# The plan of an attention and gated MLP kernel on one core: a new order of its steps, fewer fillers on TensorE, two pairs of output rows by eight products, w_out's differences in two parts

## The chip, the core and the metric

One core of a Trainium2 chip. The time is the device's time of one execution in microseconds (us), median of several executions. The engines are named as the profile names them: PE (TensorE matmuls) and PEld (its weight loads), DVE (VectorE), ACT (ScalarE), POOL (GpSimd), SP (SyncE, which issues the DMAs here).

## What is computed

```python
# attention inside chunks of 64 tokens; q, k, v are (8, 8, 576, 64)
scores = scale * np.matmul(q_c, k_c.transpose(0, 1, 2, 4, 3))
attn = np.exp(scores - max); attn = attn / (sum(attn) + 1e-09)
x = matmul(attn, v_c)              # to (8, 576, 512)
# the MLP: d_model 512, d_ff 1024
h = np.maximum(x @ w_in, 0.0)
conv_out = sum over k of conv_w[k] * h shifted by k - 1   # 3 taps along the tokens
gate = 1.0 / (1.0 + np.exp(-conv_out))
return (h * gate @ w_out).astype(np.float32)
```

q, k and v are float32; w_in, conv_w and w_out come as float64 and are split in the kernel into a high and a low part.

## The kernel before

4608 tokens are worked in tiles t0 to t35 of 128 tokens (attention) and in 12 units of 384 tokens (MLP). The kernel first writes down all work as *steps* (`step`, L80): each has an engine, a cost that the planner assumes for it, the steps that it must follow and the buffers that it takes and frees. A step's number is its place in the order of the `step` calls. A list `moved_` (L963) gives some steps to another engine than their first one, and a list `order_` (L991), both written out as numbers, gives the order in which steps are laid. From order and costs a planner (L1089 to L1129) works out a begin for each step, and the steps are emitted by their begins (L1136); so each engine's queue, SP's of DMA issues too, has a fixed order. The begins set nothing else in the chip, except this: where the planner sees PE idle in its first 110 us, it puts in transposes of a unit matrix (*fillers*, L1137 to L1140), one for each 0.14 us of the gap.

**Attention.** `load_rows` (L120) loads q and k of a tile into one of three slots, `load_v` (L171) loads v. For t0 to t8 `t_pe` (L186) turns q and k on PE, `t_copy` (L203) takes them out of PSUM; from t9 on the turning is done by `shuffle`, `load_part` and a transpose on DVE (L217). `scores` (L240) is followed by the softmax: s_max, s_sub (DVE), s_exp (ACT), s_sum, s_eps, s_rec, s_norm (DVE, ACT or POOL), then `p_pe` (PE, L326), `p_copy`, and `attn_v` (PE, L339). `x_hi` and `x_lo` (L394, L398) write x in two parts. From t12 on two tiles are worked together.

**Weights.** `split` (L650) makes of w_in (four pieces of 256 columns, the first two in two halves) a high and a low part: w_scale (ACT, L558), w_shift (DVE, L562), w_words (DVE, L567), w_hi (L76), w_left (L571). `split_o` (L676) does so with w_out and adds four sums and differences of its quarters: w_hi_q and w_lo_q (L584) for the three quarters that are used as they are, w_diff (three instructions, L589 to L591), w_hi_d and w_lo_d (L597) for the four sums and differences.

**MLP.** A block (`block`, L824) is one unit and one of eight slices of 128 hidden columns: `mm1` (12 matmuls, L408), then h_relu, c_mid (L446), c_left and c_right (L451), c_sig (L462), c_mul (L481). The output is made for pairs of 128-token tiles (`pair_steps`, L842; 18 pairs): the 2x2 blocks of h*gate and w_out are multiplied by seven products in place of eight, after Strassen and Winograd. That takes seven *factors* in two parts (f_hi, L76 or L78; f_lo, L499), four sums of blocks (f_sum, L502), seven `product` steps (12 matmuls each, L512) and o_copy, o_both, o_last, o_store. Each product waits for all steps of w_out (`w_all`, L888).

Of the kernel before, what the change touches and what calls it, by code (L numbers as in the profile page):

```python
# [20 lines left out]
F32 = mybir.dt.float32  # L21
F32R = mybir.dt.float32r
U32 = mybir.dt.uint32
# [7 lines left out]
def attn_ffn(ctx: ExitStack, tc: tile.TileContext, q, k, v, w_in, conv_w, w_out, out):  # L31
# [26 lines left out]
    DIRECT = ()  # L58
    scale = 1.0 / float(D) ** 0.5
# [12 lines left out]
    ENG = {"DVE": nc.vector, "POOL": nc.gpsimd}  # L72
# [7 lines left out]
    def step(eng, cost, key, fn, args=(), after=(), take=(), free=(), lag=0.0, port=False, bank=None, other=(), soft=()):  # L80

        s = dict(eng=eng, cost=cost, key=key, fn=fn, args=args, after=[a for a in after if a], take=take, free=free,
                 lag=lag, port=port, bank=bank, other=other, soft=[a for a in soft if a])
        steps.append(s)
        return s
# [28 lines left out]

    def row_slot(st):
        return slots[st["slot"]] if "slot" in st else w_slots[st["wslot"]][:, 0:1024]

    def load_rows(st, t):  # L120
        if t < NP:
            r = row_slot(st).rearrange("(p two) (h c) -> two p h c", two=2, h=H)
            (b0, t0), (b1, t1) = chunk(2 * t), chunk(2 * t + 1)
            for i, src in enumerate((q, k)):
                for b, t_, p0, n in [(b0, t0, 0, C)] if b0 == b1 else [(b0, t0, 0, C // 2), (b1, t1, C // 2, C // 2)]:
                    nc.sync.dma_start(out=r[i, p0:p0 + n], in_=src[b, :, t_:t_ + 2 * n, :].rearrange("h (p e) d -> p h (e d)", e=2))
# [3 lines left out]
        for i, src in enumerate((q, k)):  # L130
            rows = r[:, i].rearrange("p (h d) -> p h d", d=D)
            for b, t_, p0, n in [(b0, t0, 0, P)] if b0 == b1 else [(b0, t0, 0, C), (b1, t1, C, C)]:
                nc.sync.dma_start(out=rows[p0:p0 + n], in_=src[b, :, t_:t_ + n, :].rearrange("h i d -> i h d"))
# [37 lines left out]
    def load_v(st, t):  # L171
# [3 lines left out]
        if t >= TP:  # L175
            (b0, t0), (b1, t1) = chunk(2 * t), chunk(2 * t + 1)
            for b, t_, p0, n in [(b0, t0, 0, P)] if b0 == b1 else [(b0, t0, 0, C), (b1, t1, C, C)]:
                nc.sync.dma_start(out=r[p0:p0 + n].rearrange("p g u d -> p (g u) d"), in_=v[b, :, t_:t_ + n, :].rearrange("h j d -> j h d"))
            return
        (b0, t0), (b1, t1) = chunk(2 * t), chunk(2 * t + 1)  # L180
        for hp in range(2):
            for b, t_, j0, n in [(b0, t0, 0, P)] if b0 == b1 and not hp else [(b0, t0, C * hp, C), (b1, t1, C - C * hp, C)]:
                nc.sync.dma_start(out=r[j0:j0 + n, :, hp, :], in_=v[b, hp::2, t_:t_ + n, :].rearrange("g j d -> j g d"))
# [259 lines left out]

    def c_mid(st, u, f):
# [76 lines left out]
    def o_copy(st, row, col, eng):  # L521
        o, src = o_tile(st)[:, row, col, :], banks[st["y"]][:, 0:DM // 2]
# [10 lines left out]
    def o_last(st):  # L533
        o = st["os"][:, 1, 0, :]
        nc.vector.scalar_tensor_tensor(out=o, in0=banks[st["q"]][:, DM // 2:DM], scalar=0.5, in1=o, op0=ALU.mult, op1=ALU.add)
# [5 lines left out]
    def w_load(st, src):  # L541
        np_, n, m2 = src.shape
        t = w_slots[st["wslot"]].bitcast(U32)[0:np_, 0:n * m2].rearrange("p (n m) -> p n m", m=m2)
        nc.sync.dma_start(out=t, in_=src)
# [41 lines left out]
    def w_diff(st, n, eng):  # L586
        q_ = w_quarters(st, n)
        st["D"] = d = work4.tile([P, 2 * DM], F32, name="wt").rearrange("p (i m) -> p i m", i=4)
# [4 lines left out]
    def w_hi_d(st, n, eng):  # L593
        copy_on(eng, wo_h[:, 3:7, n], st["D"])

    def w_lo_d(st, n, eng):
        ENG[eng].tensor_tensor(out=wo_l[:, 3:7, n], in0=st["D"], in1=wo_h[:, 3:7, n].bitcast(F32), op=ALU.subtract)  # L597
# [50 lines left out]
    slot_users = []  # L648

    def split(key, t_load, src, hi=None, lo=None, half=False):  # L650

        st = {}
        small = hi is None
        a, b, c, p = (0.2, 0.28, 0.35, 0.4) if small else (0.42, 0.68, 0.62, 1.28) if half else (0.69, 1.22, 1.06, 2.35)
        ld = step("SP", 0.55, t_load, w_load, (st, src), take=[("wslot", st)], lag=0.1 if small else 1.6 if half else 3.1)
# [14 lines left out]
        s4 = step("DVE", b, key + 0.01, w_words, (st,), [s2], free=["wslot"], port=True)  # L670
        slot_users.append(s4)
# [4 lines left out]
    def split_o(n, key, t_load):  # L676

        st = {}
        ld = step("SP", 0.55, t_load, w_load, (st, src_o[n]), take=[("wslot", st)], lag=3.5)
# [5 lines left out]
        s6 = step("POOL", 2.95, key + 3, w_diff, (st, n), [s4], take=["wt"], port=True, other=[("DVE", 1.6, True)])  # L685
        s7 = step("POOL", 1.95, key + 4, w_lo_q, (st, n), [s5, s6], free=["wt"], port=True, other=[("DVE", 1.0, True)])
        s8 = step("ACT", 1.06, key + 4, w_hi_d, (st, n), [s6], other=[("POOL", 1.5, True), ("DVE", 0.7, True)])
        s9 = step("POOL", 2.4, key + 5, w_lo_d, (st, n), [s8, s7], free=["wt"], port=True, other=[("DVE", 1.25, True)])
        wo_done[n] = [s5, s7, s8, s9]

    def att(t, key, load_key, writes):

        st = {"t": t}
        if t < NAT:
            r = "slot"
            ld = step("SP", 1.2 if (2 * t) % NCK < NCK - 1 else 2.3, load_key, load_rows, (st, t), take=[(r, st)], lag=1.9 if t < NP else 2.8)
            tt = []
            for i in range(2):
                s = step("PE", 0.9 if t < NP else 0.44, key - 3, t_pe, (st, i), [ld, before.get("t")], take=[("bk", st, ("tp", i))] + ["qk"] * (not i), free=[r] if i else [])
                before["t"] = s  # L700
                tt.append(step("ACT", 0.63 if t < NP else 0.59, key - 3, t_copy, (st, i), [s], free=[("bk", ("tp", i))], other=[("DVE", 0.69, False)]))
            slot_users.append(s)
# [3 lines left out]
        ldv = step("SP", (1.7 if (2 * t) % NCK < NCK - 1 else 2.2) if t < TP else 0.5 if (2 * t) % NCK < NCK - 1 else 1.0, load_key + 0.05 if t < 5 else key - 8, load_v, (st, t), [before.get("v")], take=["v"], lag=1.1 if t < TP else 0.75 if (2 * t) % NCK < NCK - 1 else 1.2)  # L706
# [479 lines left out]
```

## Time and profile before

| | |
|---|---|
| median of 3 executions | 478.6 us (476.5 to 479.18) |
| the profiled execution | 477.3 us |
| its span, first to last instruction | 475.5 us |
| PE busy in the span | 464.0 us (98%) |
| mean granted TensorE clock | 0.996 of full speed |
| first block's first matmul | 39.75 us |
| first product's first matmul | 87.46 us |
| end of the last matmul on the chain | 471.95 us |

A busy PE is not yet a useful one: fillers count as busy. The views used are the page, the busy time by stretch, the chain that ended last, the timeline and the list of instructions by line.

### The profile page before, as it was taken

The page shows a single profiled execution, that of the slowest core. Times are in us where ns is not written, and L with a number is a line of the kernel's source. Part 1 is how long each engine was busy: PE and PEld are TensorE (multiplying, and loading weights), DVE is VectorE, ACT ScalarE, POOL GpSimd, SP SyncE. Part 2 cuts the span into 40 slices and gives each one's busy share as a digit, 9 for nine tenths or more (in the row PEclk, how much of TensorE's full clock was granted, in tenths as well). Part 3 has the DMA queues.
Part 4 walks back from the last instruction along what each step waited for, and adds up shares of the span by engine and source line. Part 5 has one row for each costly group of instructions (what it writes and reads, how often), then busy time and mean ns, then how long its engine had stood idle before and what let it go on. Part 6 is the DMA issues. An engine that isn't in the chain of part 4 may idle for free.

```text
span 475.5 us, 13438 instructions
## 1 busy us (share of the span) xinstructions
PE 464.0 (98%) x5481; PEld 452.9 (95%) x5481; DVE 413.0 (87%) x775; ACT 257.7 (54%) x535; POOL 289.4 (61%) x260
## 2 busy tenths in 40 slices
PE   8989889999999999999999999999999999999996
PEld 8879889999999999999999999999999999999996
DVE  2869999999999898989988999898998998788694
ACT  2557989955555463554564465453545545444631
POOL 0124678976777666767667857467868553633523
PEclk9989999999999999999999999999999999999999
DMA  6878999998789999999938283600361100101002
GB/s 195 237 216 255 282 207 193 188 162 205 133 143 211 200 204 160 157 228 165 221 80 149 60 208 80 166 23 23 102 167 45 46 23 2 46 1 68 8 38 112
DMA packets 186369, 64.33 MB, mean 135 GB/s; under 512 B 159660, under 2 KB 177092, under 8 KB 186308
## 3 DMA queue, kind: packets, MB, share of 16 engines
q1 hardware_dynamic: 186308, 63.48, 61.9%
q8 instruction: 43, 0.70, 0.6%
q14 instruction: 18, 0.15, 0.1%
HBM read 50.88 MB, written 23.59 MB: 157 GB/s over the span
## 4 chain that ended last, share of the span: by engine, by line
PE 89%; DVE 5%; ACT 2%; issue 2%; POOL 1%; POOLq 0%; DVEq 0%
PE b_ps L512 38%; PE b_ps L408 38%; PE sx_ps L247 3%; PE sx_ps L339 3%; PE b_ps L196 2%; PE b_ps L1140 2%; PE z_ps L339 1%; DVE wt L567 1%; PE z_ps L247 1%; PE b_ps L326 1%; DVE gt L451 1%; DVE wt L562 1%; DVE m L257 1%; ACT wt L558 0%; DVE wt L261 0%
## 5 line engine op out<-in xcount | busy, mean ns | idle before, releaser
L512 PE MATMUL b_ps<-wo_h,f 128*128 128x256 f32 x1008 | 190.6, 282 | 0.1
L512 PEld LDWEIGHTS b_ps<-wo_h,f 128*128 128x128 f32 x1008 | 158.6, 188 | 2.2 <-POOL f L78 0.7
L512 PE MATMUL b_ps<-wo_l,f 128*128 128x256 f32 x504 | 141.3, 280 | 0.6 <-issue 0.6
L451 DVE SCALAR_TENSOR_TENSOR gt<-b_ps,cw,gt 128x384 f32<-128x384 f32 (+3 forms) x208 | 116.6, 576 | 9.0 <-ACT gt L446 7.1
L499 POOL TENSOR_TENSOR f<-gt,f 128x512 fp32r<-128x512 f32 x71 | 91.8, 1298 | 29.3 <-ACT f L76 9.8
L512 PEld LDWEIGHTS b_ps<-wo_l,f 128*128 128x128 f32 x504 | 94.9, 188 | 0.3 <-issue 0.3
L408 PE MATMUL b_ps<-x_h,wi_h 128*128 128x386 f32 (+2 forms) x384 | 84.7, 342 | 0.9 <-DVE gb L481 0.9
L408 PE MATMUL b_ps<-x_l,wi_h 128*128 128x386 f32 (+2 forms) x384 | 83.3, 338 | 0.0
L408 PE MATMUL b_ps<-x_h,wi_l 128*128 128x386 f32 (+2 forms) x384 | 83.1, 338 | 0.0
L462 ACT ACTIVATE gt<-gt 128x384 f32<-128x384 f32 (+2 forms) x96 | 50.2, 523 | 43.8 <-DVE gt L451 43.6
L408 PEld LDWEIGHTS b_ps<-x_l,wi_h 128*128 128x128 f32 x384 | 68.8, 188 | 0.0
L408 PEld LDWEIGHTS b_ps<-x_h,wi_l 128*128 128x128 f32 x384 | 68.6, 188 | 0.0
L408 PEld LDWEIGHTS b_ps<-x_h,wi_h 128*128 128x128 f32 x384 | 65.7, 188 | 1.8 <-DVE gb L481 1.2
L446 ACT ACTIVATE gt<-b_ps,cw 128x384 f32<-128x384 f32 (+2 forms) x104 | 56.4, 555 | 18.0 <-DVE b_ps L418 16.3
L416 ACT ACTIVATE b_ps<-b_ps 128x386 f32<-128x386 f32 (+2 forms) x78 | 37.3, 479 | 51.5 <-PE b_ps L408 47.6
L502 POOL TENSOR_TENSOR gt<-gt 128x512 f32<-128x512 f32 x43 | 55.5, 1295 | 15.2 <-PE b_ps L408 6.0
L481 DVE SCALAR_TENSOR_TENSOR gt<-gt,b_ps 128x192 f32<-128x192 f32 (+2 forms) x120 | 47.2, 410 | 8.1 <-ACT gt L462 7.4
L78 POOL CAST f<-gt 128x512 fp32r<-128x512 f32 x42 | 25.8, 613 | 33.9 <-PE b_ps L512 24.1
L76 ACT CAST f<-gt 128x512 fp32r<-128x512 f32 x43 | 26.5, 617 | 25.2 <-PE b_ps L512 14.8
L217 DVE STREAM_TRANSPOSE qkT<-qk 128x1024 f32<-128x1024 f32 (+1 forms) x30 | 33.3, 1119 | 0.4 <-DMA qk<-rows 0.4
L524 ACT ACTIVATE wt<-b_ps 128x256 f32<-128x256 f32 x50 | 18.9, 381 | 24.9 <-PE b_ps L512 24.9
L499 POOL TENSOR_TENSOR f<-gb,f 128x512 fp32r<-128x512 f32 x14 | 18.1, 1294 | 17.8 <-ACT f L76 8.7
(96 smaller groups left out, 614.8 us busy)
## 6 DMA issues: line engine op xcount, KB each, us to landing
out<-wt SPq DMA_DIRECT2D x36, 256.0 KB, 3.7
qk<-rows SPq DMA_DIRECT2D x24, 320.0 KB, 5.0
rows<-in_k SPq DMA_DIRECT2D x12, 576.0 KB, 8.7
rows<-in_q SPq DMA_DIRECT2D x12, 576.0 KB, 8.3
qk<-rows SPq DMA_DIRECT2D x24, 256.0 KB, 4.5
v<-in_v SPq DMA_DIRECT2D x21, 256.0 KB, 5.0
w<-in_moe_w_out SPq DMA_DIRECT2D x4, 1024.0 KB, 6.1
wt<-wt SPq DMA_DIRECT2D x48, 64.0 KB, 2.0
```

Of the source, the lines that this page charges most:

```text
L76: nc.scalar.copy(out=out, in_=in_)
L78: ENG[eng].tensor_copy(out=out, in_=in_)
L217: nc.vector.transpose(out=to[:, :, i:i + n], in_=of[:, :, o:o + n])
L408: nc.tensor.matmul(h_ps[:, 0:w], lhsT=wt[:, f // 2, kt, P * (f % 2):P * (f % 2) + P], rhs=xt[:, u % NX, kt, 0:w], start=n == 0, stop=n == ...
L416: nc.scalar.activation(out=h, in_=h, func=AF.Relu)
L446: nc.scalar.mul(out=g, in_=h, mul=cw[:, FT + f:FT + f + 1])
L451: nc.vector.scalar_tensor_tensor(out=g, in0=h, scalar=w, in1=g, op0=ALU.mult, op1=ALU.add)
L462: nc.scalar.activation(out=g, in_=g, func=AF.Tanh, scale=0.5)
L481: nc.vector.scalar_tensor_tensor(out=o, in0=g, scalar=1.0, in1=hv, op0=ALU.add, op1=ALU.mult)
L499: ENG[eng].tensor_tensor(out=part(st, 1), in0=quarter(*src), in1=part(st, 0).bitcast(F32), op=ALU.subtract)
L502: ENG[eng].tensor_tensor(out=quarter(*out_), in0=quarter(*a), in1=quarter(*b), op=op)
L512: nc.tensor.matmul(o, lhsT=part(ft, a)[:, j, :], rhs=w[:, i, j, :], start=first and n == 0, stop=n == 3 * FT // 2 - 1, skip_group_check=True)
```

## The change

Five things, as the diff has them. (1) `order_` and `moved_` are replaced whole. (2) The planner's account of SP's queue is changed: a transfer is not issued before the eighth one back has landed, and the assumed transfer times (`lag`) differ; this alters only begins. (3) Fillers: a gap gets none if it is no longer than 0.3 us, else one for each 0.115 us beyond 0.3 us and one more; the first gap, from 1.4 us on, gets one for each 0.164 us. (4) `PLAIN = 2`: pairs 0 and 1 are made by eight products of the four blocks themselves. (5) w_out's differences: `w_diff` makes one of the four (128x256), which the plain products use, and the new `w_more` makes the other three; w_hi_d and w_lo_d are split in the same way. Pairs 0 and 1 wait for `wo_done` alone, later pairs for `wo_more` too. The switches `TAPS = 0` and `HOMED = ()` leave the new functions k_* and `home` unused, and every load stays on SP (`eng="SP"`).

```diff
+    PLAIN = 2
+    TAPS = 0
+    HOMED = ()
...
     def w_diff(st, n, eng):
-        ENG[eng].tensor_tensor(out=d[:, 0:2], in0=q_[:, 1::2], in1=q_[:, 0:2], op=ALU.subtract)
-        ENG[eng].tensor_tensor(out=d[:, 2], in0=q_[:, 3], in1=d[:, 0], op=ALU.subtract)
-        ENG[eng].tensor_tensor(out=d[:, 3], in0=q_[:, 2], in1=d[:, 2], op=ALU.subtract)
+        ENG[eng].tensor_tensor(out=st["D"][:, 0], in0=q_[:, 1], in1=q_[:, 0], op=ALU.subtract)
+    def w_more(st, n, eng):
+        ENG[eng].tensor_tensor(out=d[:, 1], in0=q_[:, 3], in1=q_[:, 1], op=ALU.subtract)
+        ENG[eng].tensor_tensor(out=d[:, 2], in0=d[:, 1], in1=q_[:, 0], op=ALU.add)
         ENG[eng].tensor_tensor(out=d[:, 3], in0=q_[:, 2], in1=d[:, 2], op=ALU.subtract)
...
+        if p < PLAIN:
+            ends = [factor(x, at, key + i * d, need(at)) for i, (x, at) in enumerate((("A11", a11), ("A12", a12), ("A21", a21), ("A22", a22)))]
...
+        w_all = [x for n in range(FT // 2) for x in wo_done[n] + ([] if p < PLAIN else wo_more[n])]
...
+        if p < PLAIN:
+            for row, b_ in enumerate("yq"):
+                x = mul(one, 0, at, b_, 0, True, [], [("bk", st, b_)], [])
+                c = copy(row, 1, at, [x, before["st"] if row else None], b_, **({} if row else {"take": ["wt"]}))
+                x = mul(two, 1, at + d, b_, 0, False, [c], [], [])
+                c = copy(row, 0, at + d, [x, c], b_)
+                x = mul(one, 3, at + 2 * d, b_, 1, True, [c])
+                x = mul(two, 2, at + 3 * d, b_, 1, False, [x])
+                e = step("DVE", 0.43, at + 3 * d, o_last, (st, row, 1, b_), [x, c], free=[("bk", b_)])
...
-        if e == "SP":
-            dma_free = max(dma_free, t + 0.3 + cost / 2) + s["lag"]
+        if s["lag"]:
+            ring, x = landed["SP" if e == "ACT" else e], t
+            for j in range(s["m"]):
+                x = max(x, ring[-8 + j]) + cost / s["m"]
...
-            for _ in range(int((begin[i] - pe_free) / 0.14) if idle else 0):
+            wait = begin[i] - pe_free - 0.3
+            for _ in range(int((wait + 0.3) / 0.164) if pe_free < 2.0 else int(wait / 0.115) + 1 if idle and wait > 0 else 0):
                 nc.tensor.transpose(out=banks[idle[-1]][:, 0:P], in_=ident, identity=ident)
```

What the two number lists say, read out as names. On PE up to the first product (t3 is one of a tile's two t_pe, S scores, p p_pe, A attn_v, m02 a block of unit 0 and slice 2):

```
before: t0 t0 t1 S0 t1 t2 c_pe S1 t2 t3 t3 S2 p0 t4 t4 A0 p1 S3 t5 S4 A1 t5 p2 S5 A2 p3 t6 t6
        m00 m02 m07 m03 p4 p5 S6 A3 m04 t7 m05 m06 A5 A4 m01 p6 A6 t7 S7 t8 m13 m10 m12 t8 m14 S8 m16 m11 m17 m15 p7 product
after:  t0 t0 t1 S0 t1 t2 t2 p0 S1 S2 c_pe t3 t3 S3 t4 t4 A0 p1 p2 A1 S4 t5 A2 p3 t5
        m02 S5 m07 p4 t6 t6 m03 t7 S6 t7 m00 p5 S7 A3 m05 m04 p6 A4 m01 m06 A5 A6 t8 t8 p7 S8 m16 m12 m14 m13 p8 A7 m10 A8 m15 m17 m11 product
```

SP's loads start before: rows t0, conv_w, rows t1, t2, half of a w_in piece, rows t3, half, v0, rows t4, half, rows t5, v1, two pieces, v2; after: rows t0, t1, conv_w, rows t2, half, half, rows t3, v0, rows t4, two pieces, v1, rows t5, v2. DVE's steps, before and after, counted in the list: up to the first block t_copy 5 and 2, p_copy 0 and 2, s_max 6 and 5, s_sub 6 and 5, s_sum 5 and 4, s_eps 1 and 4, s_norm 2 and 1, halves of w_shift and w_words 4 and 3; the rest alike. From there to the first product c_left 13 and 12, h_relu 0 and 1, f_lo 1 and 0, s_max, s_sub and s_sum one more each, s_rec 4 and 5, s_eps 0 and 2, s_norm 1 and 0, t_copy 0 and 1, t_dve 1 and 0, w_left of a piece 1 and of a half 0, after the reverse, w_lo_d of four quarters 1 and 0, after one w_diff, w_hi_d and w_lo_d of one quarter, a half of w_shift and w_words 0 and 1, x_lo 4 and 6; the rest alike.

## Rows read from the trace of the kernel before

**Rows 1.** The page: busy time of each engine over the span with its share and instructions, and, from the chain that ended last, its shares by engine.

```profile
PE 464.0 (98%) x5481; PEld 452.9 (95%) x5481; DVE 413.0 (87%) x775; ACT 257.7 (54%) x535; POOL 289.4 (61%) x260
...
PE 89%; DVE 5%; ACT 2%; issue 2%; POOL 1%; POOLq 0%; DVEq 0%
```

**Rows 2.** Busy time by stretch, cut by me at the places that the other groups show. Columns: the stretch, its length, then PE, PEld, DVE, ACT and POOL busy us (instructions), the granted clock, the DMA share and GB/s.

```profile
7.01:23.34 16.33, 16.33 (x441) 14.12 (x441) 11.97 (x24) 6.75 (x13) 1.89 (x2) 1.00 0.85 236
23.34:28.70 5.36, 3.55 (x66) 2.98 (x65) 1.36 (x3) 2.63 (x6) 0.94 (x1) 0.69 0.65 170
28.70:39.70 11.00, 10.27 (x195) 9.44 (x195) 10.43 (x19) 6.66 (x15) 3.52 (x6) 1.00 0.82 248
39.70:62.00 22.30, 21.05 (x241) 20.23 (x240) 21.16 (x40) 20.88 (x40) 13.86 (x14) 1.00 0.98 274
62.00:78.50 16.50, 14.51 (x176) 13.21 (x174) 16.50 (x31) 15.11 (x33) 11.03 (x9) 1.00 1.22 186
78.50:87.40 8.90, 8.90 (x59) 8.85 (x52) 8.56 (x30) 7.58 (x18) 8.74 (x9) 1.00 1.02 224
87.40:130.00 42.60, 42.60 (x593) 41.28 (x592) 38.86 (x86) 26.14 (x57) 33.83 (x31) 1.00 0.94 164
130.00:471.95 341.95, 341.18 (x3696) 337.26 (x3694) 302.47 (x543) 170.07 (x355) 214.82 (x187) 1.00 0.51 108
```

**Rows 3.** The chain that ended last, in order of time (start us, us, what), some pieces behind 78 us: four blocks of the first matmul, one product, one tile's scores, one tile's attention times V, one tile's transposes of its attention weights.

```profile
78.58 8.69 PE b_ps L408 x48
87.70 1.42 PE b_ps L512 x12
89.23 0.62 PE sx_ps L247 x32
...
91.46 0.62 PE sx_ps L339 x32
...
95.99 0.58 PE b_ps L326 x4
```

**Rows 4.** The fillers: all instructions of L1140 (durations min/median/max in ns, first and last start), and on the chain the first filler group and the first and the last of the eight filler groups (0.22 to 0.48 us each, 2.48 us together) that stand between 7.0 and 23.3 us.

```profile
L1140 PE MATMUL b_ps<-ident x112: 271/273/472, 1.4 to 93.7; 128*128 128x128 f32 x112
...
1.36 5.73 PE b_ps L1140 x35
...
8.18 0.26 PE b_ps L1140
...
21.72 0.26 PE b_ps L1140
```

**Rows 5.** The timeline of PE and DVE around the first attention times V (start us, us, engine, line, what, xcount, and in brackets the idle time before it and what ended it).

```profile
23.01 0.34 PE L339 MATMUL sx_ps<-p_all,v 64*64 64x64 f32 x6
25.15 0.88 PE L339 MATMUL sx_ps<-p_all,v 64*64 64x64 f32 x26 [1.81 <-issue]
...
27.43 1.13 PE L247 MATMUL sx_ps<-qkT 64*64 64x64 f32 x32
...
28.70 0.69 DVE L257 TENSOR_REDUCE m<-sx_ps 128x8 f32<-128x512 f32 x1 [3.97 <-PE sx_ps L247]
```

**Rows 6.** DVE's instructions up to the first product, by line (busy us, mean ns of one; then idle time before them). The first two rows keep shapes apart and reach to 90 us, the others to 87.7 us.

```profile
L567 DVE SCALAR_TENSOR_TENSOR wt<-w,wt 128x512 uint32<-128x512 uint32 x4 | 2.7, 677 | 0.1
L562 DVE TENSOR_SCALAR wt<-wt 128x512 uint32<-128x512 uint32 x4 | 1.6, 408 | 0.0
...
L451 DVE SCALAR_TENSOR_TENSOR gt<-b_ps,cw,gt 128x382 f32<-128x382 f32 (+3 forms) x32 | 15.0, 503 | 0.3 <-ACT gt L446 0.2
L257 DVE TENSOR_REDUCE m<-sx_ps 128x8 f32<-128x512 f32 x9 | 6.2, 686 | 6.3 <-PE sx_ps L247 5.9 <-PE sx_ps L339 0.3
L270 DVE TENSOR_REDUCE z<-wt 128x8 f32<-128x512 f32 x9 | 6.1, 680 | 1.1 <-ACT wt L266 1.0
L261 DVE TENSOR_TENSOR wt<-sx_ps,m 128x512 f32<-128x512 f32 x9 | 6.1, 679 | 0.2
L398 DVE TENSOR_TENSOR x_l<-sx_ps,x_h 128x512 fp32r<-128x512 f32 (+2 forms) x10 | 5.0, 524 | 0.2 <-PE sx_ps L247 0.2
L78 DVE COPY qkT<-b_ps 128x512 f32<-128x512 f32 x5 | 3.3, 677 | 1.7 <-PE b_ps L196 1.7
L217 DVE STREAM_TRANSPOSE qkT<-qk 128x1024 f32<-128x1024 f32 x1 | 1.2, 1234 | 0.0
L319 DVE TENSOR_TENSOR wt<-wt,z 128x512 f32<-128x512 f32 x3 | 2.2, 731 | 0.0
L499 DVE TENSOR_TENSOR f<-gt,f 128x512 fp32r<-128x512 f32 x1 | 1.4, 1392 | 0.0
L279 DVE RECIPROCAL z<-z 128x8 f32<-128x8 f32 x8 | 1.5, 193 | 0.3 <-ACT z L274 0.3
```

**Rows 7.** POOL's instructions of w_out's differences and of the factors, over the same time, by line and shape (same columns).

```profile
L590 POOL TENSOR_TENSOR wt<-wt 128x256 f32<-128x256 f32 x4 | 2.9, 737 | 0.3
L597 POOL TENSOR_TENSOR wo_l<-wt,wo_h 128x1024 fp32r<-128x1024 f32 x3 | 7.2, 2401 | 2.2 <-ACT wt L266 1.2 <-DVE wt L562 1.0
...
L499 POOL TENSOR_TENSOR f<-gt,f 128x512 fp32r<-128x512 f32 x71 | 91.8, 1298 | 29.3 <-ACT f L76 9.8
```

**Rows 8.** The timeline, DVE beside POOL: w_words of one 128x1024 tile at 37.32 us while POOL is idle, and another at 72.38 us.

```profile
37.32 1.23 DVE L567 SCALAR_TENSOR_TENSOR wt<-w,wt 128x1024 uint32<-128x1024 uint32 x1
...
72.38 2.05 DVE L567 SCALAR_TENSOR_TENSOR wt<-w,wt 128x1024 uint32<-128x1024 uint32 x1
```

More of the change, by code (lines that the diff above doesn't have):

```diff
@@ L78, in copy_on, with step @@
             ENG[eng].tensor_copy(out=out, in_=in_)
-    def step(eng, cost, key, fn, args=(), after=(), take=(), free=(), lag=0.0, port=False, bank=None, other=(), soft=()):
+    def step(eng, cost, key, fn, args=(), after=(), take=(), free=(), lag=0.0, port=False, bank=None, other=(), soft=(), ahead=1.1, m=1):
         s = dict(eng=eng, cost=cost, key=key, fn=fn, args=args, after=[a for a in after if a], take=take, free=free,
-                 lag=lag, port=port, bank=bank, other=other, soft=[a for a in soft if a])
+                 lag=lag, port=port, bank=bank, other=other, soft=[a for a in soft if a], ahead=ahead, m=m)
         steps.append(s)
@@ L887, in pair_steps, with mul, copy @@
         st = {}
-        w_all = [x for n in range(FT // 2) for x in wo_done[n]]
-        def mul(name, i, key, bank_, half, first, after, take=()):
+        w_all = [x for n in range(FT // 2) for x in wo_done[n] + ([] if p < PLAIN else wo_more[n])]
+        def mul(name, i, key, bank_, half, first, after, take=(), free=(("ft", "ft"),)):
             ft = fts[name]
             before["o"] = step("PE", 1.425, key, product, (st, ft, i, bank_, half, first), [ft["made"]] + w_all + after,
-                               take=list(take), free=[("ft", "ft")], soft=[before.get("o")])
+                               take=list(take), free=list(free), soft=[before.get("o")])
             return before["o"]
-        def copy(row, col, key, after, **kw):
-            return step("ACT", 0.39, key, o_copy, (st, row, col), after, other=[("DVE", 0.43, False)], **kw)
+        def copy(row, col, key, after, bank_="y", **kw):
+            return step("ACT", 0.39, key, o_copy, (st, row, col, bank_), after, other=[("DVE", 0.43, False)], **kw)
+        if p < PLAIN:
+            for row, b_ in enumerate("yq"):
+                at = key + 4 + 4 * d * row
+                one, two = f"A{row + 1}1", f"A{row + 1}2"
+                x = mul(one, 0, at, b_, 0, True, [], [("bk", st, b_)], [])
+                c = copy(row, 1, at, [x, before["st"] if row else None], b_, **({} if row else {"take": ["wt"]}))
+                if not row:
+                    before["st"] = c
+                x = mul(two, 1, at + d, b_, 0, False, [c], [], [])
[3 more added lines that the diff above has]
+                e = step("DVE", 0.43, at + 3 * d, o_last, (st, row, 1, b_), [x, c], free=[("bk", b_)])
+                last = step("SP", 0.5, key + 13 + row / 2, o_store, (st, 2 * p + row), [e, c] + ([last] if row else []),
+                            free=["wt"] if row else [], lag=0.65, ahead=5.0)
+            return
         p1 = mul("A11", 0, key + 4, "y", 0, True, [], [("bk", st, "y")])
@@ L953, in attn_ffn @@
             pair_steps(3 * (u - 1) // 2 + 2, PK[3 * (u - 1) // 2 + 2])
+    for s, f in home_next:
+        s["after"] += [home_users[i] for i in range(len(home_users)) if 1024 * i < 2 * UN * (f + 1) and 1024 * (i + 1) > 2 * UN * f]
     for s, over in x_writes:
```

177 lines of the change are left out of this document (117 added, 60 removed), and 212 rows, old and new, of tables (moved_, order_).

## The prediction

> **What bounds the kernel now.** I read the page first: PE is busy 98% of the span, and the chain that ended last lies on PE for 89% of it [rows 1]. That busy share hides the fillers, so the next view is the busy time by stretch. Behind 78.5 us PE is never idle for long: 8.90 of 8.90, 42.60 of 42.60 and 341.18 of 341.95 us [rows 2], all of it wanted work but three fillers. Ahead of 78.5 us it is not so. From 28.7 to 78.5 us DVE is busy 10.43 of 11.00, 21.16 of 22.30 and 16.50 of 16.50 us [rows 2]: there DVE sets the pace, with the splitting of the weights, the softmax and the blocks all on it. [...]
>
> So the time is a head, which ends when PE is saturated, and then PE's remaining work. An edit can gain in the head alone; each matmul that is added behind it costs its full time. The sum is made on the profiled execution, 477.3 us (span 475.5 and 1.8 around it); the median is 1.3 us above it, which I add at the end.
>
> **Term 1, DVE ahead of the first block.** The first block starts at 39.75 us, when x_lo of t2 is being written. By the lists, DVE now has less in front of it. Of what falls in the busy stretch from 28.7 us: one s_max 0.69, one s_sub 0.68, one s_sum 0.68, one half piece's w_shift and w_words 0.41 + 0.68 move behind it, and one t_copy 0.68 goes; one p_copy and one t_copy come, taken as t_copy's 0.68 each [rows 6]. Together -3.82 + 1.36 = **-2.5 us**. The further t_copy steps and the s_norm that leave DVE lay ahead of 28.7 us, where DVE waited anyway, and count nothing. Bounds: 0, if something other than DVE releases the block, and -2.5.
>
> **Term 2, DVE from there to the first product.** Both lists put 16 blocks in between. One softmax more (0.69 + 0.68 + 0.68), two x_lo (2 x 0.52), the half piece (1.09), one t_copy (0.68), one s_rec and two s_eps (3 x 0.19, the eps taken as an s_rec) make +5.4; away go the f_lo 1.39, one t_dve 1.23, one s_norm 0.73, and a w_left of a half in place of one of a piece, estimated by w_words' two shapes as 1.23 - 0.68 = 0.55, together -3.9 [rows 6, 8]. An h_relu more is taken to cancel the c_left less, and the w_lo_d of four quarters to cancel three instructions of one quarter. Net **+1.5 us**. Bounds by POOL's neighbourhood: w_words of a whole piece took 1.23 us with POOL idle and 2.05 us at 72.38 us [rows 8]; if two such stretched instructions vanish the term is -0.1, if two more come it is +3.1.
>
> **Term 3, PE behind the head.** Two pairs go from seven products to eight: 2 x 1.42 = +2.84 us on a saturated engine [rows 3]. Against it, two tiles' attn_v (2 x 0.62) and one p_pe (0.58) stand ahead of the first product now [rows 3]. Net **+1.0 us**. The products of the plain pairs read the same bank pair with copies between them; the o_copy waits are covered by blocks that the list puts between the products.
>
> **Costed at nothing.** The plain pairs need six factors and eight f_sum less. On POOL an f_lo takes 1.30 us [rows 7]; with the sums taken alike that is some 14 x 1.3 = 18 us of POOL, but behind 87 us PE is saturated, and POOL's work hides beside it (33.83 of 42.60 us busy); if that cover were gone it would be 18 us earlier factors, a gain only. w_more and the last w_hi_d and w_lo_d (three subtractions of 0.74, and about three quarters of 2.40, so 4.0 us per piece [rows 7]) move behind the first product, where they must be done before pair 2; POOL has the room. What waits behind them on POOL's queue are f_lo and s_norm; were POOL full, pair 2's factors would be late, at 1.42 us of PE per product. SP's loads are the same ones in another order (rows of t1 ahead of conv_w; two pieces of w_in ahead of v1), so a load that waits for its slot holds up what stands behind it on SP, v1 and v2 above all. The new account of the queue changes only begins. The end of the last matmul to the end of the span, 3.55 us, stays.
>
> **Term 4, the stall at 23.3 us.** PE stopped within the matmuls of one attn_v [rows 5], so no buffer or load is shown to release it, and the diff doesn't name it. The order of PE, the load on the DMA and the number of instructions ahead of it change. Bounds: it stays, 0; it goes, with it DVE's wait of 3.97 us [rows 5], -4.0; a second one, +4.0. I take half of the gain, **-2.0 us**.
>
> **Term 5, fillers.** 112 before [rows 4]. The first group of 35 ends at 7.09 us and t0's first turn starts then. Eight small groups from 8.18 to 21.98 us stand on the chain with 2.48 us [rows 4]; a lone filler takes 0.26 us there, put into a gap of 0.14 to 0.28 us as the planner saw it. Gaps up to 0.3 us now get none. Bounds: 0, if loads would have held PE as long, and -2.5; I take **-1.0 us**, nearer to nothing, since the rows of t3 and t4 can't be loaded before a slot is free. What fillers are for shows behind the stall: at the lower clock one tile's scores took 1.13 us [rows 5], where the chain has 0.62 later [rows 3]. [...]
>
> **Sum.** -2.5 + 1.5 + 1.0 - 2.0 - 1.0 = -3.0 us: 474.3 us for a profiled execution, 475.6 us for the median (-0.6%). A measurement of this kernel can tell about 0.5%, 2.4 us, from no change.
>
> **The rivals.**
> *The head gives more* (chance 0.20): the stall goes wholly and all eight filler groups were on the path, -2.5 + 1.5 + 1.0 - 4.0 - 2.5 = -6.5, so 472.1 us. For it: the head holds the fillers' 2.48 us and 3.97 us of DVE's wait. Against it: PE, DVE and the loads take turns there, and what one gives up another may hold.
> *The stall stays and the fillers were covered* (0.28): terms 4 and 5 are nothing, 0.0, so 478.6 us. For it: nothing in the diff aims at a stop with no releaser.
> *V comes late* (0.14), the case of the other side: v1 stands behind two pieces of w_in, which wait for their slots, so that attn_v of t1 and t2 start no earlier and the first block doesn't start ahead of 39.75 us. Terms 1, 4 and 5 are then nothing, +1.5 + 1.0 = +2.5, so 481.1 us. It decides from that start of the first block on: each us later is one more. Against it: the DMA share in the head is 0.65 to 0.98, so there is some room [rows 2].
> *The clock* (0.06): a gap without fillers brings a second stretch like the one from 23.3 us, whose 5.36 us at 0.69 left DVE waiting 3.97 us [rows 2, 5], in place of term 4's gain: -3.0 + 2.0 + 4.0 = +3.0, so 481.6 us. [...]
> *That it doesn't do what it says*: the lists differ from the first step on and the eight products are in the code, so this has no chance of its own.
>
> **How the numbers follow.** The forecast has 0.32; its own range is 473.5 to 477.7, so some two thirds of it (up to 476.2) are faster by over 0.5%. With the first rival and a little of the second that makes faster 0.45. The rest of the forecast and most of the second rival make 0.35 within 0.5%; V, the clock and a little of the second 0.20 slower. The range runs from 470.8, the first rival with its term 2 at -0.1, to 481.2, V's case: under 2 in 10 lie outside.
>
> **What would show it.** Term 1: the first block's start at some 35 to 36 us where the stall is gone, 37 where it stays. Terms 1, 2, 4 and 5 together: the first product at 83 to 84 us, and PE without gaps from 75 us on. Term 3: 128 products, that is 1536 matmuls of L512's successor, at 1.42 us the dozen. Term 4: no stretch between 20 and 40 us with a clock under 1. The forecast is wrong if the first block isn't earlier, or if PE has gaps behind the first product: a stall there isn't in any term, and it would show that the new order starves PE later on.

## The result: slower by 0.6%

The kernel before takes 477.23 us (median of 20 runs, 475.3 to 483.4), the changed one 480.46 us (20 runs, 477.0 to 483.1). The ratio of the runs is 1.0063, with a 95% interval of 1.0045 to 1.0080: some 3 us slower, where the prediction had 3 us faster. The profiled execution of the changed kernel took 479.5 us, span 477.7; its span is 2.2 us above the 475.5 of before, and it is this difference that the rows below account for. The executions of the changed kernel differ by the clock: the profiled one is of seven with a mean granted clock of 0.999 or 1.000 and a median of 479.5 us, and the other 13 have 0.992 to 0.996 and 480.8.

First the page of the changed kernel, answering [rows 1]: busy times, granted clock, the queue that brings instructions, the chain of waits by engine and by line, and the products.

```profile
PE 463.3 (97%) x5479; PEld 452.2 (95%) x5479; DVE 406.7 (85%) x773; ACT 258.4 (54%) x532; POOL 278.6 (58%) x257
...
PEclk9999999999999999999999999999999999999999
...
q8 instruction: 43, 0.70, 0.7%
...
PE 87%; DVE 7%; issue 2%; ACT 2%; DMA 2%; POOL 0%; POOLq 0%; DVEq 0%; ACTq 0%; SPq 0%
PE b_ps L414 39%; PE b_ps L549 38%; PE sx_ps L345 2%; PE sx_ps L253 2%; PE z_ps L345 2%; DMA w<-in_moe_w_in 2%; DVE wt L605 1%; PE b_ps L202 1%; PE b_ps L1235 1%; PE z_ps L253 1%; DVE wt L600 1%; DVE z L276 1%; DVE wt L267 1%; DVE gt L488 1%; ACT wt L596 1%
...
L549 PE MATMUL b_ps<-wo_h,f 128*128 128x256 f32 x1024 | 193.3, 283 | 1.3 <-issue 0.9
...
L549 PE MATMUL b_ps<-wo_l,f 128*128 128x256 f32 x512 | 143.9, 281 | 3.3 <-issue 3.3
```

PE's busy share falls from 98 to 97%. "issue", time in which an engine waited for nothing that the profile shows, has 2% of the chain as it had before [rows 1], so these shares don't yet show where the time went. There are 1024 + 512 = 1536 product matmuls, 128 products as the prediction counted them. The busy times by stretch, with the same stretches as [rows 2] (busy time of PE, PEld, DVE, ACT and POOL, granted clock, DMA share, GB/s):

```profile
7.01:23.34 16.33, 15.50 (x459) 14.05 (x457) 11.84 (x29) 8.13 (x15) 3.56 (x3) 1.00 0.86 259
23.34:28.70 5.36, 5.36 (x114) 4.68 (x110) 5.26 (x13) 3.94 (x7) 1.04 (x1) 1.00 0.86 202
28.70:39.70 11.00, 10.93 (x161) 9.96 (x160) 9.34 (x18) 6.83 (x13) 4.55 (x5) 1.00 0.86 237
39.70:62.00 22.30, 20.64 (x297) 18.84 (x295) 21.24 (x44) 19.84 (x43) 13.81 (x14) 1.00 0.92 277
62.00:78.50 16.50, 16.04 (x176) 15.18 (x177) 16.23 (x40) 16.05 (x37) 12.09 (x14) 1.00 1.13 162
78.50:87.40 8.90, 8.90 (x58) 8.83 (x57) 8.29 (x26) 5.51 (x14) 8.38 (x10) 1.00 1.10 230
87.40:130.00 42.60, 42.60 (x541) 41.80 (x540) 38.82 (x80) 22.93 (x50) 23.21 (x21) 1.00 1.05 174
130.00:471.95 341.95, 335.44 (x3650) 331.49 (x3649) 294.81 (x529) 173.66 (x357) 210.52 (x185) 1.00 0.50 106
```

In the head the stop is gone: the stretch from 23.34 to 28.7 us, in which PE stopped and the clock averaged 0.69 before, has PE busy for 5.36 of 5.36 us at 1.00. The loss is in the last row: PE is idle for 6.5 us of the stretch from 130 us on, where it was idle for 0.8 before. The first block and the first product, by PE's timeline (start, duration):

```profile
34.11 0.94 PE L414 MATMUL b_ps<-x_h,wi_h 128*128 128x384 f32 x4
...
82.81 0.29 PE L549 MATMUL b_ps<-wo_h,f 128*128 128x256 f32 x1
```

The first block starts at 34.11 us (39.75 before), the first product at 82.81 (87.46 before): 4.65 us are gained by then. From there to the end of the span it takes 477.7 - 82.81 = 394.9 us, where before it took 388.0: 6.9 us are lost. PE's waits behind the first product name the larger part (waiting line, what released it: us in total, times, longest). The kernel before:

```profile
PE b_ps L512 <- issue: 0.6, 1, 0.6
```

The changed kernel:

```profile
PE b_ps L549 <- issue: 4.3, 3, 1.8
PE sx_ps L253 <- issue: 1.9, 1, 1.9
PE b_ps L549 <- ACT wt L561: 0.4, 1, 0.4
```

Four stops, 6.15 us in all by the timeline (1.76, 1.56, 1.89 and 0.94, ending at 141.2, 165.0, 185.7 and 307.4 us), none with a releaser. The third, in PE's timeline:

```profile
181.51 0.28 PE L549 MATMUL b_ps<-wo_h,f 128*128 128x256 f32 x1
181.72 1.16 PE L345 MATMUL z_ps<-p_all,v 64*64 64x64 f32 x64
182.70 1.10 PE L253 MATMUL sx_ps<-qkT 64*64 64x64 f32 x62
185.69 0.27 PE L253 MATMUL sx_ps<-qkT 64*64 64x64 f32 x2 [1.89 <-issue]
185.90 0.39 PE L549 MATMUL b_ps<-wo_h,f 128*128 128x256 f32 x1
```

A burst of attention work stands there: 64 matmuls of attn_v and 64 of scores with as many weight loads, 256 instructions that take 2.1 us where PE doesn't halt among them (from 119.82 us in a_s114, for one). PE halts two matmuls short of the burst's end, so in the middle of one step: no buffer, load or semaphore of the plan lies there. It is the sort of stop that stood at 23.34 us in the kernel before [rows 5].

**Where PE halts.** If all records of PE in the trace (matmuls, weight loads and its few others) are counted up to the instruction with which it goes on, the stops fall on one place in every 256:

```
kernel    PE resumes   instructions ahead of it   remainder by 256
before        25.15               961                  193
before       166.17              4545                  193
changed      141.20              4034                  194
changed      165.02              4545                  193
changed      185.69              5057                  193
changed      307.45              7873                  193
```

The queue named "instruction" (q8 above) has 43 transfers for PE, of 16384 bytes each by the trace's DMA packets; 43 times 256 is 11008, about what PE has in records (11065), and the stops stand, to within one record, multiples of 256 apart. So a transfer is counted here as 256 instructions. The times of the transfers at the four stops, from the same packets (us):

```
PE starts on the 256 before   transfer          PE halts   goes on
136.15                        138.47 to 139.69   139.44     141.20
159.53                        162.72 to 163.66   163.46     165.02
181.39                        182.97 to 184.15   183.81     185.69
303.27                        305.06 to 306.01   306.51     307.45
```

In each the transfer moves while PE is already working on the 256 before the stop, and PE goes on 1.4 to 1.5 us behind its end. In the burst the 256 last 2.1 us; in the products 24 instructions take 1.42 us [rows 3], so 256 of them would last some 15 us by my estimate. The transfer at 97.40 us begins 1.3 us behind PE's start on the 256 before, at 96.09, but PE has work to 105.18 and goes on there without a gap (busy for 42.60 of the 42.60 us from 87.4 to 130), where the four stops cost 0.94 to 1.89 us each.

### The profile page after: what moved, and what is told of

It is laid out like the page before. It is cut to its first block, busy times and chain, and to the rows that moved or that the text cites. A ratio compares the mean times of both kernels' runs of the same rounds, so it can differ in the third digit from the quotient of the medians.

```text
span 477.7 us, 13424 instructions
## 1 busy us (share of the span) xinstructions
PE 463.3 (97%) x5479; PEld 452.2 (95%) x5479; DVE 406.7 (85%) x773; ACT 258.4 (54%) x532; POOL 278.6 (58%) x257
## 4 chain that ended last, share of the span: by engine, by line
PE 87%; DVE 7%; issue 2%; ACT 2%; DMA 2%; POOL 0%; POOLq 0%; DVEq 0%; ACTq 0%; SPq 0%
PE b_ps L414 39%; PE b_ps L549 38%; PE sx_ps L345 2%; PE sx_ps L253 2%; PE z_ps L345 2%; DMA w<-in_moe_w_in 2%; DVE wt L605 1%; PE b_ps L202 1%; PE b_ps L1235 1%; PE z_ps L253 1%; DVE wt L600 1%; DVE z L276 1%; DVE wt L267 1%; DVE gt L488 1%; ACT wt L596 1%
## 5 line engine op out<-in xcount | busy, mean ns | idle before, releaser
L549 PE MATMUL b_ps<-wo_h,f 128*128 128x256 f32 x1024 | 193.3, 283 | 1.3 <-issue 0.9
L549 PEld LDWEIGHTS b_ps<-wo_h,f 128*128 128x128 f32 x1024 | 161.3, 189 | 2.8 <-issue 1.1
L549 PE MATMUL b_ps<-wo_l,f 128*128 128x256 f32 x512 | 143.9, 281 | 3.3 <-issue 3.3
L536 POOL TENSOR_TENSOR f<-gt,f 128x512 fp32r<-128x512 f32 x68 | 87.7, 1294 | 29.7 <-DVE f L81 7.6
L549 PEld LDWEIGHTS b_ps<-wo_l,f 128*128 128x128 f32 x512 | 96.4, 188 | 3.7 <-issue 3.7
L539 POOL TENSOR_TENSOR gt<-gt 128x512 f32<-128x512 f32 x39 | 50.4, 1295 | 15.9 <-DVE f L536 9.1
L81 POOL CAST f<-gt 128x512 fp32r<-128x512 f32 x40 | 24.5, 612 | 53.0 <-PE b_ps L549 38.9
L79 ACT CAST f<-gt 128x512 fp32r<-128x512 f32 x46 | 28.3, 617 | 16.7 <-PE b_ps L549 8.2
L561 ACT ACTIVATE wt<-b_ps 128x256 f32<-128x256 f32 x47 | 17.9, 381 | 26.7 <-PE b_ps L549 23.0
L325 POOL TENSOR_TENSOR wt<-wt,z 128x512 f32<-128x512 f32 x11 | 11.5, 1044 | 33.5 <-DVE z L285 16.0
```

Of the source, the lines that this page charges most:

```text
L79: nc.scalar.copy(out=out, in_=in_)
L81: ENG[eng].tensor_copy(out=out, in_=in_)
L536: ENG[eng].tensor_tensor(out=part(st, 1), in0=quarter(*src), in1=part(st, 0).bitcast(F32), op=ALU.subtract)
L539: ENG[eng].tensor_tensor(out=quarter(*out_), in0=quarter(*a), in1=quarter(*b), op=op)
L549: nc.tensor.matmul(o, lhsT=part(ft, a)[:, j, :], rhs=w[:, i, j, :], start=first and n == 0, stop=n == 3 * FT // 2 - 1, skip_group_check=True)
```

## The experiments

**Theory A**: PE halts where one refill of 256 is used up in or just behind a burst and the next hasn't landed. The change altered how many instructions stand ahead of the bursts (26 fillers less, two products more, another order), and so where the boundaries fall; the steps that it moved have no part in the loss. **Theory B**, the prediction's own: the new order of steps or loads starves PE there. To tell them apart, instructions are added at PE's start in place of first fillers of like duration, with nothing else changed.

**First try, a poor instrument.** Small products of the identity stand in for fillers, in this form (57 for 9 in the first kernel, then 150 for 22, 6 for 1, and 42 for 9):

```diff
-            for _ in range(int((wait + 0.3) / 0.164) if pe_free < 2.0 else ...):
+            for _ in range(int((wait + 0.3) / 0.164) - 9 if pe_free < 2.0 else ...):
                 nc.tensor.transpose(out=banks[idle[-1]][:, 0:P], in_=ident, identity=ident)
+            for _ in range(57 if pe_free < 2.0 else 0):
+                nc.tensor.matmul(banks[idle[-1]][0:C, 0:C], lhsT=ident[0:C, 0:C], rhs=ident[0:C, 0:C], start=True, stop=True)
```

a_plus96: 

> The changed kernel, with 9 of the 24 fillers of the first group (0.22 us each) replaced by 57 products of 64x64 of the identity (some 0.036 us each by the 64 of L202 in 2.29 us), so that 96 more PE instructions stand ahead of everything else, in the same time. Theory A (instructions come to PE in refills of 256, and each of the four stops of 1.76, 1.56, 1.89 and 0.94 us behind the first product falls where PE has used up one refill inside or just behind a burst of 256 attention instructions and the next has not landed): with the boundary moved by 96 none lies in the first 40 instructions of a burst, the stops go, and the time is 6 us below the changed kernel's 480.5: 474.5 us, ratio to the kernel before 0.994. Theory B (the new order of the steps or of the loads starves PE there): 48 more pairs of instructions in the first 7 us change nothing; 480.5 us, 1.006, the same four stops.

a_plus256: 

> As the run with 96, but 22 fillers replaced by 150 of the small products, so 256 instructions more: a whole refill, and every boundary lies where it lay in the changed kernel. Theory A: the stops come back, 3 to 4 of them with 4 to 6 us, 480.5 us (1.006), give or take what the small products add at the start if they are slower than 0.036 us. Theory B, and also any theory by which small products at the start are good in themselves: as the run with 96.

b_plus10: 

> The kernel before, with one filler of the first group replaced by 6 small products: 10 PE instructions more. Its large bursts at 121, 140, 162, 180 and 204 us then begin 7 instructions after to 30 ahead of a boundary, like the stopped ones of the changed kernel. Theory A: two to four stops of 1 to 2 us behind the first product, 480 to 483 us (1.006 to 1.012), although nothing else is changed. Theory B: no change, 477.3 us, ratio 1.000.

a_oldfill96: 

> The changed kernel with the filler rule of the kernel before (15 more fillers in the head), and the count of the instructions ahead made the same as in the run with 96, by 42 small products for 9 fillers. So the boundaries lie as in that run and only the fillers differ. Theory A: no stops behind the first product; against the run with 96 it is later by what the fillers put back on the path, 0 to 2.5 us (1.0 in the prediction): 474.5 to 477. Theory B: the stops stay, 480.5 to 483.

Measured: 479.41 us (ratio 1.0041, 1.0022 to 1.0060), 506.64 (1.0612, 1.0582 to 1.0641), 479.35 (1.0041, 1.0018 to 1.0063) and 481.35 (1.0074, 1.0037 to 1.0111). None of these tests what it was meant to. The small products of a_oldfill96 at the start (start, duration, count):

```profile
4.75 5.34 PE L1236 MATMUL b_ps<-ident 64*64 64x64 f32 x84
```

84 matmuls for 42 products: each goes in two passes, so the instructions added were 210, 556, 22 and 180. And a pass took 5.34 / 84 = 0.064 us here, and 0.108 in a_plus256 (300 in 32.26 us), in place of 0.036, so the start was late as well: t0's first turn begins at 34.17 us in a_plus256, at 6.67 in the changed kernel. Why the two prices differ stays open. What the traces still show: the stops without a releaser behind the first product (three in a_plus256, of 1.17, 2.34 and 0.90 us, two in b_plus10, of 1.81 and 0.33, one in a_oldfill96, of 0.52) all have the remainder 193 or 194.

**Second try.** The same, with the small products in the shape that the kernel's own transposes have, in turn on the two halves of the output:

```diff
+            for j in range(29 if pe_free < 2.0 else 0):
+                nc.tensor.matmul(banks[idle[-1]][C * (j % 2):C * (j % 2) + C, 0:C], lhsT=ident[:, 0:C], rhs=ident[:, 0::2], start=True, stop=True)
```

a_s98: 

> The changed kernel, with 9 of the 24 fillers of the first group (0.22 us each) replaced by 29 products of 64x64 of the identity in turn on the two halves of the output, as L202 has them (each two passes of 0.036 us there), so 98 more PE instructions in the same 2 us. Theory A (PE's instructions come in refills of 256; the four stops of 1.76, 1.56, 1.89 and 0.94 us behind the first product fall where one refill is used up in or just behind a burst of 256 attention instructions and the next has not landed): no boundary lies in the first 40 instructions of a burst now, the stops go, the first product stays at 83 us, and the time is 6 us below 480.5: 474.5 us, ratio to the kernel before 0.994. Theory B (the new order of steps or loads starves PE there): the same four stops, 480.5 us, 1.006.

a_s256: 

> As the run with 98, but 22 fillers replaced by 75 such products (150 passes for 4.9 us of fillers): 256 instructions more, a whole refill, so each boundary lies where it lay in the changed kernel. Theory A: the stops come back where they were, 3 to 4 of them with 4 to 6 us, and the time with them: 479 to 481 us (1.004 to 1.008). If small products at the start did good by themselves, it would be 474.5 like the run with 98. Theory B: 480.5.

b_s10: 

> The kernel before, with one filler of the first group replaced by 3 such products (6 passes, 0.22 us): 10 PE instructions more, no time. The bursts at 121, 140, 162, 180 and 204 us then begin between 7 instructions behind a boundary and 30 ahead of one, like the stopped ones of the changed kernel. Theory A: two to four stops of 1 to 2 us behind the first product, 479 to 482 us (1.004 to 1.010), with nothing else changed. Theory B: 477.2 us, 1.000.

b_s212: 

> The kernel before, with 20 of its 35 first fillers replaced by 63 such products (126 passes, 4.5 us for 4.5 us): 212 instructions more, after which only the burst at 326 us, where the DMA is quiet, begins within 40 instructions of a boundary. Theory A: no stop behind the first product in place of the 0.58 us at 165.6, and none of those that other executions may have: 475.5 to 477 us (0.997 to 1.000). The run with 98 is then below this one by what the head gained: 1 to 4 us, the real worth of the change. Theory B: 477.2 us, 1.000, and the changed kernel with 98 above it by 3 us.

The small products of a_s98, 1.91 us for 57 of the passes in a row, so 0.034 each:

```profile
4.65 1.91 PE L1237 MATMUL b_ps<-ident 128*64 128x64 f32 x57
```

*a_s98*: 476.64 us, ratio 0.9983 (0.9960 to 1.0007), 3.8 us below the changed kernel. Its waits for "issue" behind the first product:

```profile
PE sx_ps L253 <- issue: 0.9, 1, 0.9
```

The stops at 139, 163, 184 and 306 us are gone, a smaller one at 279 us has come, and two in the head, of 0.78 us (16.5 us) and 1.26 us (21.9 us), all at remainder 193. Its first product is 1.8 us later than the changed kernel's (84.58 us), and it is faster all the same.

*a_s256*, a whole refill more: 480.98 us, 1.0110 (1.0066 to 1.0153), and the stops are back in their places: 1.85 us up to 142.6, 1.60 up to 185.4, 0.67 up to 306.9; only the one at 165 is down to 0.17.

```profile
PE b_ps L549 <- issue: 2.7, 3, 1.8
PE sx_ps L253 <- issue: 1.6, 1, 1.6
```

*b_s10*: three small products for one filler make the **kernel before** about as slow as the changed one: 479.87 us, 1.0062 (1.0032 to 1.0093), although its first product starts earlier (85.89 us).

```profile
PE b_ps L512 <- issue: 1.1, 1, 1.1
PE b_ps L408 <- issue: 0.9, 1, 0.9
PE b_ps L512 <- POOL f L499: 0.5, 1, 0.5
PE z_ps L247 <- issue: 0.3, 1, 0.3
```

The stops of 1.12 and 0.92 us lie at 165.1 and 185.0 us; the 0.54 us put down to POOL at 141.6 lies on a boundary too. The steps' order is that of before throughout, so theory B, which needs a new order, falls: its 477.2 us was missed by 2.7.

*b_s212* is a miss: 479.86 us, 1.0072 (1.0037 to 1.0106), where 475.5 to 477 was expected. Its 126 passes took 1.6 us longer than the fillers in whose place they stood (first transposes at 8.63 us, 7.02 before), one boundary at 231 us cost 0.60 us, and PE waited 2.1 us for the transposed P of two bursts (DVE, L316), which the kernel before didn't show.

**Third try: how much at which shift, and the fillers alone.** In a_s16, a_s48 and a_s114 small products stand for first fillers as above: 5 for 2, 14 for 4 and 34 for 11. a_oldfill_s114 takes back one part of the change:

```diff
-    pe_free, until_ = 1.4, 110.0
+    pe_free, until_ = 2.0, 110.0
...
-            wait = begin[i] - pe_free - 0.3
-            for _ in range(int((wait + 0.3) / 0.164) if pe_free < 2.0 else int(wait / 0.115) + 1 if idle and wait > 0 else 0):
+            for _ in range(int((begin[i] - pe_free) / 0.14) - (8 if pe_free == 2.0 else 0) if idle else 0):
...
+            for j in range(25 if pe_free == 2.0 else 0):
```

a_s16: 

> The changed kernel with 16 more PE instructions at the start (5 small products for 2 fillers). Theory A, with the stop at each boundary taken as 4.8 us (the 4.0 to 5.5 us that the changed kernel's four stopped refills took from the boundary before to the next instruction) less the time PE took for the 256 instructions between the two boundaries without stops: the sum behind the first product is 10.1 us at no shift, where 6.15 us were measured, so six tenths; at 16 it is the highest of all shifts, 13.0 us, so 7.8: 482 us, ratio to the kernel before 1.010. Theory B: 480.5, 1.006.

a_s48: 

> 48 more instructions (14 small products for 4 fillers). Theory A: the sum is 6.6, six tenths of it 4.0 us of stops: 478.3 us, 1.003, between the changed kernel and the run with 98. Theory B: 480.5.

a_s114: 

> 114 more instructions (34 small products for 11 fillers), where the sum has its least value, nothing behind the first product. Theory A: no stop without a releaser behind the first product, the 0.90 us at 278 us of the run with 98 gone too, and of its 1.26 us at 21.9 us none or little: 474.5 to 476.5 us, 0.995 to 0.999; this should be the fastest of all. A rival within theory A, that the head's stop only moves: 476.5, as the run with 98.

a_oldfill_s114: 

> The changed kernel with the filler rule of the kernel before (15 more fillers, all in the head) and 25 small products for 8 fillers of the first group, so that by 110 us as many instructions as with 114 have gone by. Only the fillers tell the two apart. Prediction's term 5: 1.0 us later than the run with 114 (0 to 2.5), some 476.5 us; the first product 1 us later. If the fillers were covered: the same time. Theory B has the stops back in both.

Measured: 477.77 us (0.9982, 0.9954 to 1.0011), 479.01 (1.0011, 0.9978 to 1.0044), 476.50 (0.9966, 0.9939 to 0.9992) and 476.98 (0.9985, 0.9960 to 1.0011). The shift of 114 is the fastest of all, its interval lies below 1, and behind its first product PE waits for 0.5 us in all:

```profile
PE b_ps L549 <- ACT wt L561: 0.3, 1, 0.3
PE sx_ps L253 <- issue: 0.2, 1, 0.2
```

From its trace, no two boundaries between 83 and 320 us lie less than 4.9 us apart, where the stopped ones would be 2.4 to 3.9 us apart without their stops. a_s48 lies between, with three stops of 1.03, 1.36 and 1.39 us where 4.0 us in all were expected. a_oldfill_s114 has no stop without a releaser over 0.2 us either, and one wait of 0.6 us for POOL; what it says of the fillers is told under term 5. a_s16 is a plain miss: 482 expected, 477.8 measured. So four more runs were made.

a_s0: 

> The changed kernel itself, beside the shifted ones. 480.5 us, 1.006, with three or four stops behind the first product, as first measured. If it comes out near 478, then the shift of 16 differs from it by no more than chance, and the size of the stops differs from one set of executions to another.

a_s16_again: 

> The shift of 16 again. If the spacing of the boundaries alone sets the stops: 480 to 482 us, not below the unshifted kernel. If the delay of a refill is the larger part (a stop shows only where a refill is late as well): 477 to 479, as before, with three stops of other sizes than before.

a_s114_again: 

> The shift of 114 again: 474.5 to 476.5 us, 0.995 to 0.999, no stop without a releaser over 0.3 us behind the first product; 2.5 us or more below the unshifted kernel beside it.

b_s166: 

> The kernel before at the shift where the like sum over its own trace is least (58 small products for 33 of the 35 first fillers, 166 more instructions; behind its first product 0.5 us of stops where the unshifted one has a sum of 8.6 and showed 0.58). Theory A: 476 to 477.5 us, 0.997 to 1.000: it had little to lose. The shift of 114 is then below it by the head's gain less the two products more, 1 to 3 us. If its best is as low as that of the changed kernel, the new order is worth nothing by itself.

*a_s0*, the changed kernel beside the others: 480.83 us, 1.0069 (1.0038 to 1.0101). Four stops, in the same places, 7.04 us:

```profile
PE b_ps L549 <- issue: 5.2, 3, 2.3
PE sx_ps L253 <- issue: 1.9, 1, 1.9
```

*a_s16_again*: 478.13 us, 0.9992 (0.9965 to 1.0020). So 16 instructions more really are 2.7 us better than none:

```profile
PE b_ps L549 <- issue: 3.0, 3, 1.6
```

0.51, 1.63 and 0.90 us are left of the four; that at 184 us is missing in both runs at 16. There PE needs 3.00 us for the 256, so by spacing alone it should stop; but the transfer began 0.47 us ahead of PE's start on them (0.09 us behind it in the second run), where in the changed kernel and in a_s0 it began 1.58 and 1.55 us behind. The changed kernel has such a place too: from 204.52 us PE needs 2.35 us for the 256 and doesn't stop, as the transfer began 0.81 us ahead. So at these places a stop took two things: few microseconds from one boundary to the next, and a transfer that begins late. How late it begins differs by up to 1.1 us between two runs at the same one of these places; by what rule, these runs don't settle. My sum took one delay for all boundaries, and that was wrong.

*a_s114_again*: 476.53 us, 0.9973 (0.9947 to 0.9999), with one stop of 0.96 us at 277 us, where none over 0.3 was expected: the transfer began 3.96 us behind, and the 256 lasted 5.5. Twice the fastest, and below both kernels; it is the version to keep.

*b_s166*: 477.03 us, 1.0002 (0.9976 to 1.0029), the kernel before without stops. Its waits behind the first product, and its first block and first product:

```profile
PE z_ps L339 <- DVE p_all L316: 1.7, 1, 1.7
PE sx_ps L339 <- DVE p_all L316: 0.8, 1, 0.8
PE b_ps L512 <- issue: 0.3, 1, 0.3
```

```profile
36.92 0.95 PE L408 MATMUL b_ps<-x_h,wi_h 128*128 128x384 f32 x4
...
84.63 0.36 PE L512 MATMUL b_ps<-wo_h,f 128*128 128x256 f32 x1
```

No stop without a releaser over 0.3 us is left behind the first product, and with 0.41 us at 19.7 in place of the 1.81 at 23 us the first product starts at 84.63 us in place of 87.46. But 2.5 us of waiting for P come in their place, and the time stays that of before. Why P is late in this kernel, in b_s212 and in b_plus10, and not in the kernel before, stays open.

Over all: in the profiles of the two kernels compared and of all those above but a_plus96 there are 32 stops of 0.3 us and more without a releaser behind the first product, and all 32 have the remainder 193 or 194. By chance two places in 256 would hold hardly one. The profiled execution of a_plus96, left out because it took 487.1 us where the median was 479.4, has two such stops, with the same remainder.

## Why the prediction was wrong

**The head came out near the forecast in sum.** First block: -5.64 us, for -5.5 by terms 1, 4 and 5 together. Term 1 was not measured by itself. By one profile each, b_s166 (first block at 36.92 us) puts 2.8 of it on the stop, and a_oldfill_s114 beside a_s114 (36.13 and 35.01 us) puts 1.1 on the fillers, which would leave 1.7 for the 2.5 of term 1. First block to first product, term 2: 47.71 us before, 48.70 after, so +1.0 for +1.5. That is the size and not the mechanism: where the term counts DVE's steps, the chain of the changed kernel goes through a load of w_in, until ACT starts on it at 37.26 us.

```profile
29.71 7.45 DMA w<-in_moe_w_in
```

The head was to give -4.0 in all and gave -4.65.

**Term 3 was right.** 1536 matmuls, and in a_s114, without stops, 472.2 - 83.72 = 388.5 us follow the first product, against 388.0 - 0.58 = 387.4 in the kernel before without its own: +1.1 for +1.0. What was costed at nothing behind the head stayed hidden: PE's waits there, but for the stops, are 0.4 us for ACT.

**Term 5 is not settled.** The old rule's first product, then that of the new rule at the same count of instructions:

```profile
84.91 0.28 PE L549 MATMUL b_ps<-wo_h,f 128*128 128x256 f32 x1
```

```profile
83.72 0.28 PE L549 MATMUL b_ps<-wo_h,f 128*128 128x256 f32 x1
```

1.2 us for 1.0, but from one profile each, and in a_s16 and a_s16_again, the same kernel twice, the first product lies at 83.25 and 84.67 us. In the medians it is 0.5 us (476.98 and 476.50), and their intervals overlap.

**The step that failed is term 4, and with it the split into a head, where alone an edit can gain, and PE's remaining work behind it, where PE was taken to have no gaps.** The stop at 23.34 us was taken for one of the head: it stays, goes or comes a second time, with half its gain as forecast and its sign looked for between 20 and 40 us. The term named the number of instructions ahead as one thing that changes, and didn't ask where else in the program PE could halt in the same way; such stops behind the first product stand in the sum at nothing, and they went from 0.58 to 6.15 us. In the head the stop is worth 2.8 us in the profile of before (first product 87.46, in b_s166 84.63), so its size was well within bounds; but it isn't bound to the head or to the order: it shrinks by a shift alone in b_s166, and in the changed kernel four boundaries behind the first product came to lie where PE halts. The profile's difference is -4.65 for the head, +1.1 for term 3 and 6.15 - 0.58 = +5.6 for the stops, +2.0 of the 2.2 measured. Two numbers beside the sum were off as well: the first rival with its term 2 at -0.1 gives 470.5, not 470.8, and the 1.3 us from profile to median came from 3 executions; with 20 the median of the kernel before is 477.23 us, not 478.6.

**The rivals.** V did not come late in the profile: the first block is 5.6 us earlier, and that 481.1 us is near the result is no more than that. The clock is at 1.00 in every stretch of the profile with 26 fillers less, so no gap left open is seen to take it down, and no run shows what the clock rival assumed of such a gap. Behind some of the stops the clock is lower. In a_s0 the granted clock is 0.50 from 142.0 to 145.0 us, at the end of a stop, and again from 169.5 to 172.5, behind the one that ends at 167.88; before, it is 0.50 from 25.5 to 28.5, behind the stop of 1.81 us. At the first of these a product's matmul takes 0.58 us in place of 0.28:

```profile
142.48 0.58 PE L549 MATMUL b_ps<-wo_l,f 128*128 128x256 f32 x1 [2.34 <-issue]
```

At the second two of them in a row take 0.63 us in place of 0.40. Not each stop does it: the four in the profile of the changed kernel, up to 1.89 us, left the clock at 1.00. So these two stops of a_s0 cost more than their own length, and the 13 executions of the changed kernel at a lower clock would fit that; with 114 instructions more, the 12 of a_s114 all have 0.998 or more. No rival had a stop behind the first product; the last sentence of the prediction has it as what would make it wrong, and that is what came, though not because the order starves PE.

**What the change is worth without stops** is less than forecast, and the runs don't fix it: by medians 0.5 us (476.53 for a_s114_again, 477.03 for b_s166), by ratios 0.9973 and 1.0002, so 1.4 us, with intervals of some 1.2 us either way on each.

## What to carry to other kernels

Where PE halts without a releaser, count its instructions up to where it goes on. Here the remainder by 256 repeated, 193 or 194 at all 32 stops, so the stops hung on the position in the instruction stream, and small edits ahead of them changed them: 10 instructions more made the one of 0.58 us into 1.12 and brought one of 0.92 (b_s10), 98 more took four away behind the first product and brought one of 0.90 there (a_s98). A change of under 1% in a kernel with dense bursts on PE is then judged at two or three shifts (a few tiny matmuls at an idle place of the start) before its gain or loss is put down to what it does. And a stop that vanishes with an edit has perhaps only moved: the forecast needs a term for where it can come up again.

## What the runs showed of the hardware

- The instruction queue made 43 transfers of 16384 bytes for PE's 11065 records, some 257 to one, and the 32 stops lie at one place, remainder 193 or 194, in every 256 records; they took 0.3 to 2.6 us each. Ten instructions more at the start made the kernel before 2.8 us slower (b_s10, 479.87 for 477.04 beside it), 114 more made the changed one 4.3 us faster (a_s114_again, 476.53 for 480.83 of a_s0).
- From the end of the transfer to PE's next instruction it took 1.4 to 1.5 us at the four stops of the changed kernel; the transfers themselves took 0.94 to 1.22 us.
- Behind some of these stops the granted clock was 0.50 (a_s0, 142.0 to 145.0 and 169.5 to 172.5 us), behind others it stayed at 1.00 (all four in the profile of the changed kernel).
- An f32 product of 64x64 went in two passes (84 matmuls for 42 products in a_oldfill96). In a row on the same half of the output they took 0.064 us each in a_oldfill96 and 0.108 in a_plus256; with the halves in turn and all 128 rows used, 0.034 (a_s98).
